# Moving the issue of one value load from SyncE's queue to ScalarE's, in a one-core attention and MLP kernel

## The chip, the cores and the metric

The kernel runs on one core of one Trainium2 chip. The metric is device time in microseconds (us), lower is better. PE is TensorE, ACT is ScalarE, DVE is VectorE, POOL is GpSimd and SP is SyncE; a "q" behind a name (SPq, ACTq) marks the instructions by which that engine issues DMAs.

## The reference

Attention over 4 batches, 8 heads, 768 positions and a head size of 64, and then a two-layer MLP on its 3072 tokens:

```
scores = q @ k^T / 8          # per batch and head, 768 x 768
heads 0, 2, 6 ("retrieval"):  causal mask
heads 1, 3, 4, 5, 7 ("streaming"): causal, and only the first 4 keys or the last 64
a = softmax(scores); x = a @ v          # heads side by side: 3072 x 512
h = x @ w_in                            # 512 -> 2048
out = (max(h, 0) + alpha * min(h, 0)) @ w_out   # 2048 -> 512
```

Inputs and output are float32; inside, the kernel multiplies in bfloat16.

## The kernel before

The heads are worked off in pairs, (2, 6), (1, 5), (0, 4), (3, 7), for each of the 4 batches, so there are 16 pairs, n = 0 to 15; batch 0 holds pairs 0 to 3. For each pair the kernel loads queries (`Lq`), keys (`Lk`) and values (`Lv`) as float32, casts them to bfloat16 (`Cq`, `Ck`, `Cv`), transposes queries and keys on PE (`Tq`, `Tk`, copied out of PSUM by `tq`, `tk`), multiplies keys with queries into PSUM (`S`), takes the exponential on ACT (`s`), multiplies with the values on PE (`A`), divides by the row sum on DVE (`a`), and transposes the result into the MLP's layout (`X`, `x`). The MLP is `P` (first layer), `p` and `g` (activation on ACT and DVE), `O` (second layer) and `o` (output).

The order of all this is written out by hand: `ORDER` (line 14) is one list of items, and the loop at line 807 emits them in that order. An engine executes its own instructions in the order in which they were emitted; engines wait for each other through semaphores only. An item name such as `s0.1.0` reads: exponential, pair 0, second head, part 0.

What the change and the prediction touch:

- `load_v(n)` (line 227) calls `load_rows` (line 230), which issues one DMA for each of the pair's two heads, on SP. Pair 2 is heads 0 and 4. Head 0's values are 128 x 6 x 64 float32 (192 KB), and head 4's are 128 x 7 x 64 float32 (224 KB): a streaming head is cut into 7 tiles, each 124 rows behind the one before it. Both are cut into runs of 256 bytes.
- All loads of queries, keys and values are issued on SP, but for one: the first head's keys of pair 0, on ACT (line 223). ACT also issues the small load of the slopes (line 727) in front of it, and, in the last microseconds, two output tiles.
- In `ORDER`, `Lv2` stands behind `Lq3` (the fourth pair's queries) and in front of `Lv3`. On SP's queue this gives: Lv1 (two DMAs), Lq3 (one), Lv2 (two), Lv3 (two), Lq5, Lk4, and so on.
- `E_retr` (line 466) and `E_stream` (line 513) are the exponentials. In batch 0 the scores of a part take a pair of PSUM banks, and there are two such pairs, `SC2 = [(0, 1), (2, 3)]` (line 292). An exponential gives its pair of banks back, so the scores two parts further on wait for it.
- `cast_v` (line 347) casts the values of pairs 0 to 2 on POOL, and for a streaming head copies the four sink rows into the other tiles (`sinks`, line 301). POOL also casts the queries and keys of pairs 1 to 3, and issues the loads of the MLP's weights (line 693).
- DMAs from SP and ACT use eight completion semaphores in turn, and each waits until the DMA that last used its semaphore is complete.

On ACT the exponentials around the change stand in this order: `s1.1.0`, `s1.0.0` (pair 1), then `s0.1.0`, `s0.1.1`, `s0.1.2` (pair 0, second head), then the copy `tq2`. On PE, the scores `S0.1.2` need the banks that `s0.1.0` gives back, and `A0.1` multiplies what the three exponentials wrote.

Of the kernel before, what the change touches and what calls it, by code (L numbers as in the profile page):

```python
# [14 lines left out]
vz2 id busy warm4 warm0 warm5 vz0 qz0 Lq0.0 sz2 so2 Lq0.1 zero vz3 nms Lk1 Lq1 sz1 Cq0.1 nmr Ck1.1 kz1 La Lk0 Ck1.0  # L15
kz0 Cq1 Cq0.0 Tq0.0 Ck0.0 Tk0.0 tk0.0 Lk2 Ck2.0 Lv0 warm2 tq0.0 S0.0.0 s0.0.0 qz S0.0.1 Tk1 warm3 warm6 vo kz2 Ck0.1
vz1 Ck2.1 Tq1 s0.0.1 tq1 Tq0.1 tk1.1 S0.0.2 s0.0.2 Cv0 tk1.0 m4.0.2 warm7 tq0.1 Lq2 S1.1.0 Tk0.1 tk0.1 S1.0.0 ro0
s1.1.0 Tk2 tk2.1 idf Cq2 s1.0.0 S0.1.0 s0.1.0 A0.0 S0.1.1 s0.1.1 S0.1.2 Tq2 warm8 s0.1.2 tq2 S1.1.1 s1.1.1 A0.1 kz3
sz0 Lk3 Ck3.1 Lv1 S1.0.1 m4.1.2 a0.0 s1.0.1 Al Ck3.0 Lq3 tk2.0 Tk3 S2.0.1 s2.0.1 a0.1 tk3.1 al X0 x0 S2.0.2 Lv2 Lv3
so1 so0 Lq5 wi1 s2.0.2 Lk4 m8.0.2 wi0 Cq3 Tq3 S2.0.0 s2.0.0 tk3.0 Cv1 tq3 A1.0 a1.0 Lk5 kfz2 A1.1 a1.1 kfz0 S2.1.0  # L20
S2.1.1 Cv2 s2.1.1 kfz3 wi6 A2.0 a2.0 wi7 S3.1.0 s2.1.0 s3.1.0 wi5 wi4 S3.0.0 A2.1 Cv3.0 s3.0.0 X1 S3.1.1 s3.1.1 S3.0.1
a2.1 X2 x1 x2 m8.1.2 near2 Ck4.0 P0.0.0 wi2 s3.0.1 A3.0 Cv3.1 P0.3.0 a3.0 P0.2.0 P0.2.1 A3.1 Ck4.1 Lk7 Lk6 P0.1.0
P0.1.1 P0.0.1 Tk4 tk4.0 Cq5 m14.0.2 a3.1 X3 nz1 tk4.1 x3 Tq5 P0.3.1 tq5 P1.2 p1.2 P1.0 p1.0 g1.0 P0.1.2 wi3 P0.13 Lq4
# [51 lines left out]
def kernel(  # L75
# [13 lines left out]
    nc = tc.nc  # L89
    B, H, S, D = q.shape  # L90
# [76 lines left out]
    vf = [stat.tile([128, 7, 2, 64], fp32, name=f"vf{i}") for i in range(NF)]  # L167
# [25 lines left out]
    def dram(t, offset, dims):  # L193
        return bass.AP(t.tensor, t.offset + offset, dims)

    def heads(n):
        return PAIRS[n % 4]
# [17 lines left out]
    def load_k(n):  # L215
        if n >= CROSS:
            load_rows(n, k, kf)
            return
        for hh, h in enumerate(heads(n)):
            T = row_tokens(n, h)  # L220
            dst = kf[n % NF].rearrange("p a b d -> p (a b d)")[:, 6 * D * hh:6 * D * (hh + 1)]

            (nc.scalar if n == hh == 0 else nc.sync).dma_start(
                dst.rearrange("p (x y) -> p x y", y=T * D),
                dram(k, (n // 4 * H + h) * S * D, [[T * D, 128], [128 * T * D, 6 // T], [1, T * D]]))

    def load_v(n):
        load_rows(n, v, vf)

    def load_rows(n, src, bufs):  # L230

        dst = bufs[n % NF]
        for hh, h in enumerate(heads(n)):
            o = (n // 4 * H + h) * S * D
            if n >= LAY and not RETR[h]:

                end = o + 112 * NT * D > B * H * S * D
                nt = NT - end
                nc.sync.dma_start(dst[NSINK:116, 0:nt, hh, :], dram(src, o, [[D, 112], [112 * D, nt], [1, D]]))
                if end:  # L240
                    nc.sync.dma_start(dst[NSINK:100, 6, hh, :], dram(src, o + 672 * D, [[D, 96], [1, D]]))
                (nc.gpsimd if n == 13 and src is k else nc.sync).dma_start(
                    dst[0:NSINK, :, hh, :], dram(src, o, [[D, NSINK], [0, NT], [1, D]]))
                continue
            nt, step = (6, 128) if RETR[h] else (7, 124)
            nc.sync.dma_start(dst[:, 0:nt, hh, :], dram(src, o, [[D, 128], [step * D, nt], [1, D]]))


    ident = const.tile([128, 128], bf16, name="ident")
# [37 lines left out]
    def item(name, fn, *args):  # L287
        I[name] = lambda: fn(*args)
# [67 lines left out]
    def to_array(key, nat, choices, first_half=False):  # L356

        held[key] = take(*choices)
        tr = bank_bf(held[key][0])
        for i in range(6):  # L360
            if first_half:
                nc.tensor.transpose(tr[0:D, 128 * i:128 * (i + 1)], nat[:, i, 0:D], ident)  # L362
            else:
                nc.tensor.transpose(tr[:, 128 * i:128 * (i + 1)], nat[:, i, :], ident)  # L364
# [382 lines left out]
    for n in range(NSEG):  # L747
        if n:
            item(f"Lq{n}", load_q, n)
            item(f"Cq{n}", cast_q, n)  # L750
        item(f"Lk{n}", load_k, n)
        item(f"Lv{n}", load_v, n)
        if n == 3:
            for hh in range(2):
                item(f"Cv{n}.{hh}", cast_v_head, n, hh)
        else:
            item(f"Cv{n}", cast_v, n)
        if n < CROSS:
            for hh in range(2):
                item(f"Ck{n}.{hh}", cast_k, n, hh)  # L760
            if n:
                two = [(4,), (5,)] if n < 4 else ANY
                item(f"Tq{n}", lambda n=n, two=two: to_array(("q", n), natq[n], two))
                item(f"tq{n}", put_q, ("q", n), n, slice(0, 128), "A")
                item(f"Tk{n}", lambda n=n, two=two: to_array(("k", n), natk[n], two))
                for hh in range(2):
                    item(f"tk{n}.{hh}", put_k, ("k", n), n, hh, True)
        else:
            item(f"Ck{n}", cast_k_near, n)
            item(f"Dq{n}", dma_q, n)  # L770
            for hh in range(2):
                item(f"Dk{n}.{hh}", dma_k, n, hh)
        for hh, h in enumerate(heads(n)):
            k_ = (3 if n < 4 else 6) if RETR[h] else (2 if n < 4 else 3)
            for m in range(k_):
                item(f"S{n}.{hh}.{m}", S_retr if RETR[h] else S_stream, n, hh, m)
                item(f"s{n}.{hh}.{m}", E_retr if RETR[h] else E_stream, n, hh, m)
                if n >= 4:
                    item(f"m{n}.{hh}.{m}", M_retr if RETR[h] else M_stream, n, hh, m)
            item(f"A{n}.{hh}", AV, n, hh)  # L780
            item(f"a{n}.{hh}", AV_out, n, hh)
        if LAY <= n < NSEG - 1:
            item(f"X{n}", X_dma, n)
        else:
            item(f"X{n}", X_pe, n)
            item(f"x{n}", X_out, n)
# [61 lines left out]
```

## Time and profile before

| | us |
|---|---|
| median of 3 runs | 228.52 |
| lowest and highest run | 228.26 and 229.8 |
| the profiled execution, its own time | 228.43 |
| its span, from the first to the last instruction | 225.8 |
| PE busy in the span | 221.6 (98%) |
| DVE, ACT, POOL busy | 149.1, 140.1, 45.9 |

The profiled execution's own time is 2.6 us longer than its span; that part lies around the instructions and is in every run. Times in the views below count from the start of the span. The change is in the stretch from 13 to 18 us of the span. In a row of the timeline the first number is when the instructions begin, the second how long they take (a merged row: from the first begin to the last end), then engine, line and operation, with the tiles written and read; behind it, in brackets, how long the engine was idle before and what ended that. The row of an instruction that issues a DMA is the time of the issue, not of the transfer.

### The profile page before, as it was taken

The page shows a single profiled execution, that of the slowest core. Times are in us where ns is not written, and L with a number is a line of the kernel's source. Part 1 is how long each engine was busy: PE and PEld are TensorE (multiplying, and loading weights), DVE is VectorE, ACT ScalarE, POOL GpSimd, SP SyncE. Part 2 cuts the span into 40 slices and gives each one's busy share as a digit, 9 for nine tenths or more (in the row PEclk, how much of TensorE's full clock was granted, in tenths as well). Part 3 has the DMA queues.
Part 4 walks back from the last instruction along what each step waited for, and adds up shares of the span by engine and source line. Part 5 has one row for each costly group of instructions (what it writes and reads, how often), then busy time and mean ns, then how long its engine had stood idle before and what let it go on. Part 6 is the DMA issues. An engine that isn't in the chain of part 4 may idle for free.

```text
span 225.8 us, 5241 instructions
## 1 busy us (share of the span) xinstructions
PE 221.6 (98%) x2005; PEld 136.5 (60%) x2005; DVE 149.1 (66%) x393; ACT 140.1 (62%) x286; POOL 45.9 (20%) x91
## 2 busy tenths in 40 slices
PE   7999999999999999999999999999999999999994
PEld 7989876575556557564556455456556555664454
DVE  5798648986659618897899029977486536866000
ACT  3788669999898036587992147786584237563311
POOL 5679749600230001000400001000110100000000
PEclk9999999999999999999999999999999999999999
DMA  6999999999999999999989999976924420000213
GB/s 201 311 240 214 281 223 285 197 196 231 204 284 182 117 232 231 170 167 190 268 160 177 226 243 129 238 156 117 119 94 38 120 93 0 0 3 1 93 68 119
DMA packets 95417, 37.39 MB, mean 166 GB/s; under 512 B 82440, under 2 KB 93600, under 8 KB 95392
## 3 DMA queue, kind: packets, MB, share of 16 engines
q1 hardware_dynamic: 89136, 27.73, 65.2%
q0 software_dynamic: 5792, 8.93, 17.5%
q10 hardware_dynamic: 464, 0.40, 0.6%
q8 instruction: 15, 0.25, 0.5%
q14 instruction: 10, 0.08, 0.1%
HBM read 27.71 MB, written 6.29 MB: 151 GB/s over the span
## 4 chain that ended last, share of the span: by engine, by line
PE 98%; DVE 0%; issue 0%; DVEq 0%
PE P L598 37%; PE P L618 36%; PE P L553 7%; PE P L431 4%; PE P L414 3%; PE P L688 3%; PE P L364 2%; PE P L637 2%; PE P L424 1%; PE P L502 1%; PE P L578 1%; PE P L463 0%; PE P L362 0%; DVE kT L387 0%; DVE ot L646 0%
## 5 line engine op out<-in xcount | busy, mean ns | idle before, releaser
L610 DVE SCALAR_TENSOR_TENSOR g<-neg,oma,P 128x256 bf16<-128x256 f32 (+1 forms) x128 | 70.9, 608 | 36.9 <-ACT neg L603 36.4
L598 PE MATMUL P<-xT,w_in_b 128*128 128x512 bf16 (+1 forms) x512 | 86.6, 326 | 0.0
L618 PE MATMUL P<-w_out_b,g 128*128 128x512 bf16 x368 | 85.3, 379 | 0.0
L603 ACT ACTIVATE neg<-P 128x512 f32<-128x512 f32 x96 | 54.2, 600 | 26.3 <-PE P L598 20.9
L598 PEld LDWEIGHTS <-w_in_b 128*128 128x128 bf16 x512 | 49.5, 98 | 32.3 <-DVE g L610 0.2
L618 PEld LDWEIGHTS <-g 128*128 128x128 bf16 x368 | 33.9, 98 | 37.2 <-issue 1.0
L470 ACT ACTIVATE eR<-P 128x448 bf16<-128x448 f32 (+4 forms) x63 | 36.9, 635 | 5.8 <-PE P L431 2.5
L624 ACT COPY ot<-P 128x512 f32<-128x512 f32 x23 | 13.9, 605 | 37.1 <-PE P L618 32.3
L628 POOL DMA_DIRECT2D out_dram<-ot x18 | 10.3, 572 | 111.0 <-ACT ot L624 110.8
L518 ACT ACTIVATE eS<-P 128x352 bf16<-128x352 f32 x45 | 20.8, 489 | 3.4 <-PE P L431 3.0
L564 DVE TENSOR_TENSOR xn<-P,rcp 128x448 bf16<-128x448 f32 (+1 forms) x32 | 19.5, 608 | 1.1
L529 DVE TENSOR_TENSOR eS<-eS,ms_near 128x352 bf16<-128x352 bf16 x45 | 14.9, 346 | 0.6 <-ACT eS L518 0.5
L563 DVE RECIPROCAL rcp<-P 128x7 f32<-128x7 f32 (+1 forms) x32 | 6.3, 198 | 10.9 <-PE P L553 10.8
L480 DVE TENSOR_TENSOR eR<-eR,mr_near 128x128 bf16<-128x128 bf16 (+5 forms) x54 | 10.7, 227 | 4.3 <-ACT eR L470 4.1
L414 PE MATMUL P<-qT,kT 128*128 128x192 bf16 (+14 forms) x68 | 11.2, 251 | 0.2 <-DVE kT L387 0.2
L553 PEld LDWEIGHTS <-eS 128*128 128x128 bf16 x260 | 9.5, 97 | 2.3 <-issue 0.6
L553 PE MATMUL P<-vb,eS 128*128 128x65 bf16 x260 | 10.7, 193 | 0.0
L431 PE MATMUL P<-qT,kT 64*128 64x176 bf16 (+10 forms) x168 | 10.5, 252 | 0.0
L431 PEld LDWEIGHTS <-kT 64*128 64x128 bf16 x168 | 6.7, 94 | 6.2 <-issue 5.5
L553 PE MATMUL P<-vb,eR 128*128 128x65 bf16 x276 | 10.5, 193 | 0.0
L553 PEld LDWEIGHTS <-eR 128*128 128x128 bf16 x276 | 9.5, 97 | 1.3
L646 DVE COPY ot<-P 128x128 f32<-128x128 f32 x1 | 0.3, 291 | 14.3 <-PE P L637 14.3
(95 smaller groups left out, 177.3 us busy)
## 6 DMA issues: line engine op xcount, KB each, us to landing
out_dram<-ot POOLq DMA_DIRECT2D x18, 256.0 KB, 3.9
kf<-in_k_dram SPq DMA_DIRECT2D x21, 192.0 KB
qf<-in_q_dram SPq DMA_DIRECT2D x18, 192.0 KB
vf<-in_v_dram SPq DMA_DIRECT2D x14, 196.0 KB
qf<-in_q_dram SPq DMA_DIRECT2D x7, 384.0 KB
vf<-in_v_dram SPq DMA_DIRECT2D x12, 192.0 KB
w_in_b<-in_moe_w_in_dram POOLq DMA_DIRECT2D x8, 256.0 KB, 9.6
w_out_b<-in_moe_w_out_dram POOLq DMA_DIRECT2D x4, 512.0 KB, 13.9
```

The source lines that it names most:

```text
L414: nc.tensor.matmul(to, keys, queries, start=True, stop=stop)
L431: nc.tensor.matmul(to, keys[own], queries[own], start=True, stop=True)
L470: nc.scalar.activation(ebuf[n, hh][:, lo:hi].rearrange("p (x c) -> p x c", x=len(parts)), P[:, got[0]:got[0] + len(parts), 0:(hi - lo) // ...
L518: nc.scalar.activation(slots, sc[:, 0:352].rearrange("p (s c) -> p s c", c=176), AF.Exp, scale=scale)
L529: nc.vector.tensor_tensor(slots, slots, ms_near[:, 0:2, :] if m == 0 else ms_near[:, 1:3, :], op=ALU.mult)
L553: nc.tensor.matmul(pav[:, i, :], e[:, o:o + 128], vv[:, j, hh, 0:D + 1], start=(m == 0), stop=(m == len(terms) - 1))
L564: nc.vector.tensor_tensor(xn[n][:, 0:nt, D * hh:D * hh + D], pav[:, :, 0:D], rcp.to_broadcast([128, nt, D]), op=ALU.mult)
L598: nc.tensor.matmul(psg[:, w * i:w * (i + 1)], w_in_b[:, c, 128 * fb:128 * (fb + 1)], xT[:, c, o:o + w], start=(x == 0), stop=(x == 3))
L603: nc.scalar.activation(neg[t, f], bank(held["P", t, f][0]), AF.Relu, scale=-1.0)
L610: nc.vector.scalar_tensor_tensor(g_buf[t % 2][:, fb, 0:w], neg[t, f][:, c], oma[:, fb:fb + 1], bank(got[0])[:, c], op0=ALU.mult, op1=ALU.add)
L618: nc.tensor.matmul(bank(held["O", t, s][0]), g_buf[t % 2][:, f, 128 * s:128 * (s + 1)], w_out_b[:, f, :], start=(f == 0), stop=(f == 15))
L624: nc.scalar.copy(ot, bank(got[0]))
```

## The change

The load of pair 2's values is split into two items, one for each head. The first head's (`Lv2.0`) keeps its place in the list and its queue. The second head's (`Lv2.1`, 224 KB) is issued by ACT instead of SP, and stands in the list directly in front of `s0.1.0`, which puts it between `s1.0.0` and `s0.1.0` on ACT. Nothing else moves: PE, DVE and POOL have the same instructions in the same order. The moved DMA keeps its completion semaphore, the one that the second head's values of pair 0 (`Lv0`) used before it, and has to wait for that load and for nothing else.

```diff
 ORDER
-s1.1.0 Tk2 tk2.1 idf Cq2 s1.0.0 S0.1.0 s0.1.0 A0.0 ...
+s1.1.0 Tk2 tk2.1 idf Cq2 s1.0.0 S0.1.0 Lv2.1 s0.1.0 A0.0 ...
...
-... X0 x0 S2.0.2 Lv2 Lv3
+... X0 x0 S2.0.2 Lv2.0 Lv3
...
-    def load_v(n):
-        load_rows(n, v, vf)
+    def load_v(n, of=range(2)):
+        load_rows(n, v, vf, of)

-    def load_rows(n, src, bufs):
+    def load_rows(n, src, bufs, of=range(2)):
         dst = bufs[n % NF]
-        for hh, h in enumerate(heads(n)):
+        for hh in of:
+            h = heads(n)[hh]
...
             nt, step = (6, 128) if RETR[h] else (7, 124)
-            nc.sync.dma_start(dst[:, 0:nt, hh, :], dram(src, o, [[D, 128], [step * D, nt], [1, D]]))
+            (nc.scalar if (n, hh) == (2, 1) else nc.sync).dma_start(
+                dst[:, 0:nt, hh, :], dram(src, o, [[D, 128], [step * D, nt], [1, D]]))
...
-        item(f"Lv{n}", load_v, n)
+        if n == 2:
+            for hh in range(2):
+                item(f"Lv{n}.{hh}", load_v, n, [hh])
+        else:
+            item(f"Lv{n}", load_v, n)
```

More of the change, by code (lines that the diff above doesn't have):

```diff
@@ L17 @@
 vz1 Ck2.1 Tq1 s0.0.1 tq1 Tq0.1 tk1.1 S0.0.2 s0.0.2 Cv0 tk1.0 m4.0.2 warm7 tq0.1 Lq2 S1.1.0 Tk0.1 tk0.1 S1.0.0 ro0
-s1.1.0 Tk2 tk2.1 idf Cq2 s1.0.0 S0.1.0 s0.1.0 A0.0 S0.1.1 s0.1.1 S0.1.2 Tq2 warm8 s0.1.2 tq2 S1.1.1 s1.1.1 A0.1 kz3
-sz0 Lk3 Ck3.1 Lv1 S1.0.1 m4.1.2 a0.0 s1.0.1 Al Ck3.0 Lq3 tk2.0 Tk3 S2.0.1 s2.0.1 a0.1 tk3.1 al X0 x0 S2.0.2 Lv2 Lv3
-so1 so0 Lq5 wi1 s2.0.2 Lk4 m8.0.2 wi0 Cq3 Tq3 S2.0.0 s2.0.0 tk3.0 Cv1 tq3 A1.0 a1.0 Lk5 kfz2 A1.1 a1.1 kfz0 S2.1.0
+s1.1.0 Tk2 tk2.1 idf Cq2 s1.0.0 S0.1.0 Lv2.1 s0.1.0 A0.0 S0.1.1 s0.1.1 S0.1.2 Tq2 warm8 s0.1.2 tq2 S1.1.1 s1.1.1 A0.1
+kz3 sz0 Lk3 Ck3.1 Lv1 S1.0.1 m4.1.2 a0.0 s1.0.1 Al Ck3.0 Lq3 tk2.0 Tk3 S2.0.1 s2.0.1 a0.1 tk3.1 al X0 x0 S2.0.2 Lv2.0
+Lv3 so1 so0 Lq5 wi1 s2.0.2 Lk4 m8.0.2 wi0 Cq3 Tq3 S2.0.0 s2.0.0 tk3.0 Cv1 tq3 A1.0 a1.0 Lk5 kfz2 A1.1 a1.1 kfz0 S2.1.0
 S2.1.1 Cv2 s2.1.1 kfz3 wi6 A2.0 a2.0 wi7 S3.1.0 s2.1.0 s3.1.0 wi5 wi4 S3.0.0 A2.1 Cv3.0 s3.0.0 X1 S3.1.1 s3.1.1 S3.0.1
```

## The prediction

> **What bounds the kernel now.** I read the page first: its chain of work that ended last, and then the same chain in order of time, to see how closely PE's instructions follow each other where the change is made and much later.
>
> ```profile
> PE 98%; DVE 0%; issue 0%; DVEq 0%
> ```
>
> ```profile
> 26.67 1.08 PE P L598 x5
> ...
> 28.14 0.86 PE P L598 x4
> ```
>
> ```profile
> 130.50 16.44 PE P L598 x92
> ```
>
> PE makes up 98% of the chain. Four first-layer matmuls at 28.14 us take 0.86 us, five at 26.67 take 1.08, both 0.215 us each; no other group in the chain that I looked at runs at a faster pace for that size (the 92 at 130.50 mix the 512-column and the 256-column form, 0.179 each). So already at 26 us PE is at the pace that it keeps for the rest of the run. Two things follow. A load that lands earlier is worth nothing unless PE is waiting for it; and a stall of PE in the stage of the change is added to the end, as nothing behind it can be made up. The next view is therefore the timeline of the stage, engine by engine: ACT, PE, SP and POOL.
>
> ```profile
> 12.22 0.81 ACT L524 ACTIVATE eS<-P 128x768 bf16<-128x768 f32 x1 [0.18 <-PE P L502]
> 13.39 0.92 ACT L470 ACTIVATE eR<-P 128x896 bf16<-128x896 f32 x1 [0.36 <-PE P L463]
> 14.46 1.73 ACT L470 ACTIVATE eR<-P 128x896 bf16<-128x896 f32 x2 [0.15 <-PE P L463]
> 16.07 0.81 ACT L369 COPY qT<-P 128x768 bf16<-128x768 bf16 x1
> ```
>
> ```profile
> 14.20 0.22 PE L463 MATMUL P<-nmr,ident 128*128 128x128 bf16 x1
> 14.36 0.35 PE L414 MATMUL P<-qT,kT 128*128 128x128 bf16 x2
> ...
> 15.81 0.96 PE L553 MATMUL P<-vb,eR 128*128 128x65 bf16 x21
> ```
>
> The ACT rows are s1.0.0, then s0.1.0, then s0.1.1 with s0.1.2, then tq2. The moved DMA goes between the first two. ACT is idle there for 0.36 us, and again for 0.15 before s0.1.1. On PE, the row at 14.36 is part of the scores S0.1.2. It begins 0.16 us behind the row before it, and s0.1.0, which gives its banks back, ends at 13.39 + 0.92 = 14.31: PE is already waiting for this exponential, with no slack. The row at 15.81 is A0.1: 21 matmuls in 0.96 us, where the same 21 of A0.0 take 0.80 at 13.19; the 0.16 are a wait for s0.1.2.
>
> ```profile
> 9.48 2.06 SPq L246 DMA_DIRECT2D vf<-in_v_dram  x2
> 11.58 2.26 SPq L209 DMA_DIRECT2D qf<-in_q_dram  x1
> 13.88 3.32 SPq L246 DMA_DIRECT2D vf<-in_v_dram  x4
> ```
>
> ```profile
> 0.81 0.42 ACTq L288 DMA_DIRECT2D alpha_r<-in_moe_alpha_dram  x1
> 0.81 0.86 SPq L288 DMA_DIRECT2D qf<-in_q_dram  x2
> 1.26 0.44 ACTq L223 DMA_DIRECT2D kf<-in_k_dram  x1
> ```
>
> SP issues almost without a pause, and its issues are of very unequal length. At the start two take 0.86 us together. Lq3 takes 2.26, from 11.58 to 13.84, though it has nothing left to wait for: it is held up. ACT comes to the moved issue at 12.22 + 0.81 = 13.03, in the middle of that. ACT's own two issues took 0.42 and 0.44, beside SP's, when nothing held either of them up.
>
> ```profile
> 13.50:14.00 0.50, 0.50 (x18) 0.42 (x14) 0.49 (x2) 0.50 (x1) 0.50 (x2) 1.00 1.08 176
> 14.00:14.50 0.50, 0.50 (x6) 0.36 (x5) 0.50 (x3) 0.35 (x2) 0.50 (x2) 1.00 0.43 80
> 14.50:15.00 0.50, 0.50 (x10) 0.45 (x9) 0.47 (x4) 0.50 (x1) 0.50 (x2) 1.00 1.08 114
> ```
>
> The last column is GB/s moved by DMA: 176, 80 and 114, where the half microseconds from 10.5 to 12 moved over 300. While SP is held up in Lq3 the DMA engines run dry.
>
> **The change part by part.** *SP loses one issue.* Seen alone, Lv2.1 is the row from 14.40 to 14.94, so 0.54 us. SP's later issues can start up to 0.54 us earlier. The first time that any engine waits for one of those loads is POOL at 25.80, for keys, after 1.27 us of idleness. PE reaches what POOL casts there at 28.84, straight from P L598 at full pace. The gain to the end is 0; what hides it is PE's own work.
>
> *The values come earlier.* POOL casts them (Cv2) at 19.69, without a wait. Gain 0.
>
> *The DMA of 224 KB shares the engines with what SP has queued.* At the 307 GB/s of 11.5 to 12.0 it is worth 229 KB / 307 = 0.75 us, so Lk3, Lv1 and Lq3 can land 0 to 0.75 us later. POOL casts Lq3 at 17.04 and Lv1 at 17.80 to 18.8, and its two sink copies end at 19.45. PE takes the queries at 18.92, 1.03 us behind the end of the cast at 17.89, and begins A1.0 at 19.75, 0.30 behind the second sink copy. Bounds: 0, and 0.75 - 0.30 = 0.45 if all of it reaches POOL and the first matmul needs both copies. It needs only the first head's, so I take 0. If PE is itself late by 0.45 or more, this is hidden.
>
> *ACT gains one issue.* It does not wait for its semaphore: pair 0's values had landed when POOL cast them at 11.06. The trace has no ACT issue while SP is held up, so the length is bounded. From below: 0.44, ACT's own row for a load of keys. Then ACT is free at 13.47 instead of 13.39, and s0.1.0 is 0.08 late, which the idle 0.15 behind it takes up: 0 at the end. From above: 2.41, the longest SP issue before this point (Lq2, from 5.91). Then ACT is free at 15.44, 2.05 late. Between: ACT is held until SP is through, at 13.84, and then needs its own 0.44: 14.28, so s0.1.0 is 0.89 late. I take this one. The row nearest in time is SP's own issue beside it, which is held up then, and the two ACT rows come from a moment in which no issue was.
>
> *What is queued behind it.* s0.1.0 ends at 14.28 + 0.92 = 15.20. S0.1.2 on PE is 0.89 late. s0.1.1 begins at 15.20 instead of 14.46: 0.74, since the idle 0.15 is used up. s0.1.2 and tq2 follow back to back, 0.74 late. A0.1 arrives 0.89 late at its wait, of which 0.16 exist already; s0.1.2 lets it go 0.74 late. So PE loses 0.74 us here, and behind it has nothing that could absorb it. POOL, DVE and SP are then early in relation to PE, and wait a little longer.
>
> Sum: 0 + 0 + 0 + 0.74. On the profiled execution's own time: 228.43 + 0.74 = 229.17. The profiled time is 0.09 below the median of the runs shown, 228.52. I say **229.2 us**, 0.3% slower than before, which is inside the 1% that a measurement of this kernel can tell from no change.
>
> The Trainium skill, Perfetto Trace Analysis, section DMA Instruction — HWDGE (DVE, Sync), says that a DMA of this kind first takes an exclusive lock on a descriptor generator, and that the time until it has the lock is inside the recorded issue. By that rule ACT would wait for the end of Lq3, and the sum would be the 229.2; without it, by ACT's own row, 228.5. The start of this trace shows both queues issuing at once with no sign of the lock (0.42 beside 0.86 for two), so no row here decides it.
>
> **The rivals.** *ACT is not held up.* For it: 0.42 and 0.44 beside SP's issues. Against: no issue was held up then. It gives 228.43 + 0 to 0.1, so about 228.5, not slower; with all of the late landing, 228.9. It decides once the issue takes less than 13.39 + 0.15 - 13.03 = 0.51 us.
>
> *SP gets the next turn as well.* SP's following issue begins only 0.04 us behind Lq3 and lasts 0.47, until 14.35. If ACT comes after it, it ends at 14.79, s0.1.0 is 1.40 late and PE 1.25: 229.7.
>
> *ACT is held for as long as the longest issue,* because its own descriptors do not fit: 2.05 late, PE 1.90, 230.3, with 2.68 (the longest issue in the first 30 us) 230.6. Only with some further loss would this pass 230.8, over 1%.
>
> *A gain.* PE's waits in the stage, 0.16 at 14.20 to 14.36 and 0.16 in A0.1, are for ACT, which the change cannot make earlier. If the earlier loads removed as much elsewhere: 228.1. Against it: from 15 to 35 us PE shows no idle time at all.
>
> **How the numbers follow.** Held until SP is through: 0.48. Not held: 0.34. SP has the next turn as well: 0.09. Held for the longest time: 0.06, half of it or less beyond 1%. A gain: 0.03. The likeliest gives 229.2; its own range is 229.0 to 229.4. The range of 228.3 to 229.8 takes in the first three cases. Faster by over 1% has 0.01, as no row offers 2.3 us; slower by over 1% has 0.03; within 1% is 0.96.
>
> **What would show it.** In the profile after: an ACTq row of line 247 from 13.03 with 1.2 to 1.3 us (right) or about 0.5 (not held); s0.1.0 at 14.3 and not 13.4; the row of S0.1.2 at 15.2; A0.0 to A0.1 drawn out; DMA still below 180 GB/s in 13.5 to 15 if held, near 300 if not. A cast of Lq3 on POOL behind a wait for DMA would show the shared engines. The prediction is wrong if the ACTq row is short, or if it is long and PE's later groups still begin at their old times.

## The result and the profile after

| | before | after |
|---|---|---|
| median of 22 runs each, us | 228.30 | 228.95 |
| lowest and highest run, us | 227.35 and 231.08 | 228.49 and 230.6 |
| ratio, with its 95% interval | | 1.0041 [1.0023, 1.0059] |
| the profiled execution's own time, us | 228.43 | 229.06 |

The change costs 0.4%, about 0.9 us. Of the experiments below, the profiles of the extra copy and of the load later on ACT are of slow runs, which every ratio leaves out (the medians do not): of these two profiles what waits for what is read, and a size in them is that of one execution. Line 246 of the code is line 247 in the changed kernel, and the lines behind it are numbered 2 higher (8 higher in the two kernels with parts of the load).

ACT's timeline around the moved issue, after:

```profile
11.84 0.81 ACT L526 ACTIVATE eS<-P 128x768 bf16<-128x768 f32 x1 [0.18 <-PE P L504]
11.85 0.42 ACTq L247 DMA_DIRECT2D vf<-in_v_dram  x1
12.67 0.92 ACT L472 ACTIVATE eR<-P 128x896 bf16<-128x896 f32 x1
```

The issue is short, 0.42, and it lies wholly inside the exponential `s1.0.0`: it begins 0.01 us behind it and is over 0.38 us before that ends. `s0.1.0` follows at 12.67 with no idle time at all. So the issue takes nothing from ACT. SP's timeline shows that SP was held up in Lq3 at the same moment:

```profile
11.79 1.66 SPq L209 DMA_DIRECT2D qf<-in_q_dram  x1
```

The loss is on POOL and then on PE. POOL's timeline shows the cast of Lq3, here before:

```profile
17.04 0.85 POOL L315 CAST g<-qf 128x768 bf16<-128x768 f32 x1
```

And after, with the two sink copies of Lv1, which follow behind the cast of Lv1:

```profile
18.46 0.83 POOL L317 CAST g<-qf 128x768 bf16<-128x768 f32 x1 [1.67 <-DMA qf<-in_q_dram]
...
20.23 0.63 POOL L308 COPY vb<-vb 4x192 f32<-4x192 f32 x2
```

Before, the cast found its queries there. After, POOL was idle for 1.67 us and a DMA into `qf` ended that: the cast begins 1.42 us later (18.46 against 17.04). By the trace's DMA records the last packet of Lq3 ended at 17.80 instead of 16.46, so 1.34 later; the cast began 0.66 us behind it, and 0.58 in the kernel before, where Lq3 was thus only just in time. All that POOL does behind it moves by the same 1.4 us. Now PE's timeline, before and then after: Tq3 (the row with `g`), A1.0 and the scores behind it. After, the last group ahead of Tq3 stands in front; before, the same group began at 18.86.

```profile
18.92 0.50 PE L364 MATMUL P<-ident,g 128*128 128x128 bf16 x6
...
19.75 0.95 PE L553 MATMUL P<-vb,eS 128*128 128x65 bf16 x26
20.54 0.24 PE L414 MATMUL P<-qT,kT 128*128 128x192 bf16 x1
```

```profile
18.14 0.23 PE L465 MATMUL P<-nmr,ident 128*128 128x144 bf16 x1
19.34 0.51 PE L366 MATMUL P<-ident,g 128*128 128x128 bf16 x6 [0.97 <-POOL g L317]
...
20.22 0.22 PE L555 MATMUL P<-vb,eS 128*128 128x65 bf16 x2
20.62 0.89 PE L555 MATMUL P<-vb,eS 128*128 128x65 bf16 x24 [0.18 <-POOL vb L308]
21.34 0.24 PE L416 MATMUL P<-qT,kT 128*128 128x192 bf16 x1
```

Before, PE goes from group to group and does the 26 matmuls of A1.0 in one piece. After, it waits twice: 18.14 to 19.34 for Tq3, 1.14 us more than the 0.06 step between the same two groups before, and inside A1.0 from 20.22 to 20.62, after two matmuls, until the first sink copy is done. The second wait is 0.40 - 0.06 = 0.34.

The two waits add up to 1.48, but PE is only 0.80 behind at the next group (21.34 against 20.54). It had come to this place 0.72 us earlier than before (18.14 against 18.86). That is jitter of the first loads: in two experiments with the same work in front, below, the same group began at 18.56 (five tiles) and 19.43 (values cast first). It is also worth nothing here, since A1.0 cannot go on until POOL's copy is ready at 20.6, however early PE stands there. So the sum is simple. The copy is ready 2.12 us behind the start of the cast of Lq3 (20.23 + 0.35 = 20.58, from the row below, less 18.46). With the cast at 17.04 that was 19.16, and PE passed this point at about 19.81 (19.75 and two matmuls): slack 0.65. The delay of 1.42 less 0.65 makes 0.77, against 0.80 seen.

The chain of waits of the changed kernel, in order of time, now runs through POOL where it was all PE:

```profile
18.48 0.81 POOL g L317
...
20.23 0.35 POOL vb L308
20.62 0.89 PE P L555 x24
```

And far behind it, the chain's row with 32 second-layer matmuls, which began at 123.59 before:

```profile
124.29 6.91 PE P L620 x32
```

The stall is carried along to the end: 0.70 later here, and also 0.70 later at the last DVE instruction (223.55 against 222.85).

Why Lq3 lands later is seen in the DMA of the stretch from 13.5 to 15.5, in half microseconds (last column GB/s), after:

```profile
13.50:14.00 0.50, 0.50 (x7) 0.40 (x6) 0.47 (x4) 0.35 (x2) 0.50 (x2) 1.00 1.06 207
14.00:14.50 0.50, 0.50 (x12) 0.49 (x10) 0.50 (x2) 0.50 (x1) 0.50 (x2) 1.00 1.33 252
14.50:15.00 0.50, 0.50 (x12) 0.50 (x10) 0.41 (x4) 0.50 (x2) 0.50 (x3) 1.00 1.32 229
15.00:15.50 0.50, 0.50 (x14) 0.40 (x12) 0.50 (x2) 0.50 (x2) 0.50 (x2) 1.00 1.17 235
```

The hole of before (176, 80, 114) is filled, at 231 GB/s on average. What fills it is the 224 KB: by the trace's DMA records ACT's queue moved 169 KB from 14 to 15 us, and SP's 66. The first packet of ACT's queue began at 13.33, the first of Lq3 at 14.83. Two things in this are easily missed. The load on ACT was not issued ahead of Lq3: its issue began 0.06 us behind Lq3's (11.85 and 11.79), and it overtook Lq3 on its own queue. And its transfer did wait: the first packet came 1.06 us behind the end of its issue (12.27), at about the time at which SP's issue of Lq3 ended (13.45).

### The profile page after: what moved, and what is told of

Read it like the earlier page. It is cut to its first block, busy times and chain, and to the rows that moved or that the text cites. A ratio compares the mean times of both kernels' runs of the same rounds, so it can differ in the third digit from the quotient of the medians.

```text
span 226.9 us, 5213 instructions
## 1 busy us (share of the span) xinstructions
PE 219.5 (97%) x1977; PEld 135.8 (60%) x2005; DVE 149.6 (66%) x393; ACT 140.3 (62%) x286; POOL 46.1 (20%) x91
## 4 chain that ended last, share of the span: by engine, by line
PE 89%; DMA 3%; POOL 3%; SPq 2%; issue 2%; DVE 0%; POOLq 0%; DVEq 0%
PE P L600 36%; PE P L620 35%; PE P L555 7%; PE P L433 4%; DMA qf<-in_q_dram 3%; PE P L639 2%; PE P L426 1%; PE P L366 1%; SPq L223 1%; POOL g L317 1%; PE P L580 1%; PE P L416 1%; PE P L504 1%; POOL w_in_b L695 1%; SPq L247 0%
## 5 line engine op out<-in xcount | busy, mean ns | idle before, releaser
L600 PE MATMUL P<-xT,w_in_b 128*128 128x256 bf16 (+1 forms) x501 | 85.7, 325 | 0.6
L620 PE MATMUL P<-w_out_b,g 128*128 128x512 bf16 x351 | 83.1, 379 | 1.0 <-issue 0.2
```

The costliest lines, as they stand in the source:

```text
L600: nc.tensor.matmul(psg[:, w * i:w * (i + 1)], w_in_b[:, c, 128 * fb:128 * (fb + 1)], xT[:, c, o:o + w], start=(x == 0), stop=(x == 3))
L620: nc.tensor.matmul(bank(held["O", t, s][0]), g_buf[t % 2][:, f, 128 * s:128 * (s + 1)], w_out_b[:, f, :], start=(f == 0), stop=(f == 15))
```

## The experiments

The theory after the result: what costs time is that 224 KB are served in front of Lq3, on whatever queue; Lq3 lands later, POOL casts it later, and PE waits at Tq3 and A1.0. The rivals: ACT pays for issuing a DMA (as the prediction had it); or a second queue takes more than its share of the DMA engines from SP's.

**Only an issue, and nothing to move.** To the kernel before, an extra load of 8 KB on ACT at the same place.

```diff
+    item("La2", nc.scalar.dma_start, extra, moe_alpha...)    # 16 x 128 float32
-s1.0.0 S0.1.0 s0.1.0
+s1.0.0 S0.1.0 La2 s0.1.0
```

> The kernel before, with one more DMA on ACT in front of s0.1.0, of 8 KB (the slopes again, into a spare tile that nobody reads). All loads stay on SP. Theory (shared DMA engines): an issue of about 0.42 us on ACT that delays nothing, ratio 1.000 within 0.002. Rival (the issue on ACT costs): ratio 1.003 to 1.005 with s0.1.0 late by 0.1 us or more.

228.28 us, ratio 1.0006 [0.9975, 1.0037]. The issue and the exponential behind it, in ACT's timeline:

```profile
12.42 0.33 ACTq L288 DMA_DIRECT2D extra<-in_moe_alpha_dram  x1
13.24 0.92 ACT L470 ACTIVATE eR<-P 128x896 bf16<-128x896 f32 x1
```

SP was inside its own issue of Lq3 (12.10 to 13.81). The issue costs ACT nothing in these rows, so the rival that ACT pays falls; the interval by itself does not exclude its 1.003.

**Only the traffic.** To the kernel before, an extra copy of the same 224 KB on ACT at the same place, into a tile that nobody reads; Lv2 stays on SP.

```diff
+    item("Lx", nc.scalar.dma_start, extra, dram(v, 4 * S * D, [[D, 128], [124 * D, 7], [1, D]]))
-s1.0.0 S0.1.0 s0.1.0
+s1.0.0 S0.1.0 Lx s0.1.0
```

> The kernel before, with all its loads on SP, and a second copy of the same 224 KB issued on ACT in front of s0.1.0 into a spare tile that nobody reads. It takes nothing off SP. Theory (shared DMA engines): Lq3 lands 1 us or more later, PE waits at Tq3 for POOL's cast by 0.7 to 1.5 us, ratio 1.003 to 1.007, no better than the change. Rival (what costs is that SP's later loads come in another order): no wait at Tq3, ratio 1.000 to 1.002.

229.08 us, ratio 1.0066 [1.0033, 1.0099]. POOL's timeline:

```profile
18.70 0.83 POOL L315 CAST g<-qf 128x768 bf16<-128x768 f32 x1 [1.75 <-DMA qf<-in_q_dram]
...
29.61 0.50 POOL L328 CAST natm<-kf 128x384 bf16<-128x384 f32 x1 [3.15 <-DMA kf<-in_k_dram]
```

The traffic alone brings the whole delay of the cast. PE waits 0.31 us more than usual at Tq3, less than expected because it came there later, and 0.34 at A1.0. In this profile the cast of keys at 29.61 waits 3.15 too; that the 224 KB which the kernel does not need are the cause is not shown, as the kernel before with `Lq3` first (below) waits 2.61 at the same cast without them.

**The same position on SP's queue.** The changed kernel with the moved load on SP, in front of Lq3.

```diff
-            (nc.scalar if (n, hh) == (2, 1) else nc.sync).dma_start(
+            nc.sync.dma_start(
-S0.1.0 Lv2.1 s0.1.0
+S0.1.0 s0.1.0
-Ck3.0 Lq3
+Ck3.0 Lv2.1 Lq3
```

> The moved load goes back to SP, but in front of Lq3 instead of behind Lv2's first head: the early place without ACT. Theory (224 KB served in front of Lq3, whatever the queue): Lq3 lands 0.7 to 1.5 us later than in the kernel before, PE waits at Tq3, ratio 1.003 to 1.008. Rival (a second queue beside SP's takes an unfair share of the DMA engines, and in one queue there is no harm): ratio 1.000 to 1.002.

228.98 us, ratio 1.0049 [1.0021, 1.0078], against 1.0041 of the changed kernel. POOL's timeline, and then PE's:

```profile
18.81 0.83 POOL L317 CAST g<-qf 128x768 bf16<-128x768 f32 x1 [1.59 <-DMA qf<-in_q_dram]
```

```profile
20.97 0.88 PE L555 MATMUL P<-vb,eS 128*128 128x65 bf16 x24 [0.18 <-POOL vb L308]
```

Without ACT, and with one queue, the loss is the same within the intervals. So the loss needs no second queue, and what matters is that the 224 KB are served in front of Lq3. On ACT it is the second queue that brings them there, since they are issued behind Lq3: by 0.06 us in the changed kernel, by 1.14 with the extra copy (12.59 and 11.45). The rival falls as the cause of the loss, but whether ACT's queue also takes more than its share is not settled.

**Lq3 out of the way.** The changed kernel with Lq3 in front of Lv1 on SP, so that it is issued before the moved load; and the kernel before with the same swap, to see what the swap is worth by itself.

```diff
-sz0 Lk3 Ck3.1 Lv1 S1.0.1 m4.1.2 a0.0 s1.0.1 Al Ck3.0 Lq3 tk2.0
+sz0 Lk3 Ck3.1 Lq3 Lv1 S1.0.1 m4.1.2 a0.0 s1.0.1 Al Ck3.0 tk2.0
```

> The changed kernel, with the fourth pair's queries Lq3 issued on SP in front of Lv1 instead of behind it. The moved load stays on ACT where the change put it. Theory (PE pays only because Lq3 lands behind the 224 KB): Lq3 lands 1 us or more earlier, POOL's cast of it no longer waits, PE begins Tq3 without idleness, and the time goes back to that of the kernel before or a little below, ratio 0.997 to 1.001. Rival (the 224 KB delay every load by the same amount, so some other wait takes its place, Lv1 first): a wait of PE in A1.0 of 0.5 to 1 us, ratio 1.003 to 1.005.

> The kernel before, with Lq3 in front of Lv1 on SP; all loads on SP. It separates the swap's own worth from what it mends in the changed kernel. Theory: in the kernel before Lq3 is only just in time, so the swap is worth 0 to 0.3 us in most executions, ratio 0.997 to 1.001. Rival (the swap is good or bad in itself): ratio below 0.997 or above 1.003.

With the change 228.34 us, ratio 1.0022 [0.9996, 1.0049]; without it 228.29, 1.0019 [0.9989, 1.0050]. POOL in the kernel with the change:

```profile
16.95 0.85 POOL L317 CAST g<-qf 128x768 bf16<-128x768 f32 x1
```

The cast has no wait, PE none at Tq3 and A1.0, and with the swap on both sides the change no longer shows in the time (1.0022 beside 1.0019). The two intervals together leave about 0.9 us open between these two, as much as the change costs, so it is the rows that show it more than the times. Both ratios lie above the 0.997 to 1.001 that had been expected: the swap may cost something itself, but both intervals hold 1.

**Parts of the load.** The changed kernel, but ACT issues only the first three tiles (96 KB), or the first five (160 KB); SP issues the others behind `Lv2.0`.

```diff
-            for hh in range(2):
-                item(f"Lv{n}.{hh}", load_v, n, [hh])
+            item("Lv2.0", load_v, n, [0])
+            item("Lv2.1", load_v, n, [1], (0, 3))       # or (0, 5), on ACT
+            item("Lv2.1r", load_v, n, [1], (3, 7))      # or (5, 7), on SP
```

> The changed kernel, with only three of the seven tiles (96 of 224 KB) on ACT at the early place, the other four (128 KB) on SP behind Lv2's first head. Theory (bytes in front of Lq3): about three sevenths of the delay, Lq3 0.4 to 0.7 us late instead of 1.4, PE's wait at Tq3 0 to 0.5 us, ratio 1.001 to 1.003. Rival (one more queue costs, whatever its size): ratio 1.004 as with the change.

> The changed kernel, but ScalarE issues only five of the seven tiles of the moved load (160 of 224 KB) at the early place; SyncE issues the other two behind Lq3. Theory of the shared engines (Lq3 lands later by what is served in front of it): with 96 KB the cast of Lq3 began 0.5 us later than before (17.53), with 224 KB 1.42 us later (18.46), so by interpolation 160 KB puts it near 18.0, behind a wait for DMA of about 1.2 us. That is 0.95 us late against PE's slack of 1.03 at Tq3: PE waits there for at most 0.2 us, and at A1.0 for 0.1 to 0.35 behind the sink copies. Ratio 1.000 to 1.003. Rival (the cost hangs on how many loads stand in front, and not on their size): cast as late as in the changed kernel, 18.4 or later, PE waits 1 us and 0.34, ratio 1.004.

Three tiles: 227.94 us, ratio 0.9984 [0.9958, 1.0011]. Five: 228.30, 0.9999 [0.9970, 1.0028]. POOL with three tiles, then with five, and PE with five (timelines):

```profile
17.53 0.83 POOL L323 CAST g<-qf 128x768 bf16<-128x768 f32 x1 [0.52 <-DMA qf<-in_q_dram]
```

```profile
18.23 0.83 POOL L323 CAST g<-qf 128x768 bf16<-128x768 f32 x1 [1.46 <-DMA qf<-in_q_dram]
```

```profile
20.39 0.89 PE L561 MATMUL P<-vb,eS 128*128 128x65 bf16 x24 [0.18 <-POOL vb L314]
```

The cast moves with the size, and the price begins only when the slack is used up. With 96 KB the copy is ready at 17.53 + 2.12 = 19.65, before PE's 19.81: no cost is due, and none is measured, where a tenth of a per cent or more had been expected. With 160 KB this profile stands at 20.39, so 0.58 late; the runs give 0.00, with up to 0.6 us inside the interval. That the cost at 160 KB is smaller than at 224 is likely, though the two intervals touch (up to 1.0028, and from 1.0023 on); its size is open. The cast had been expected near 18.0 and began at 18.23.

**Queries on ACT, values on SP.** The kernel before with Lq3 issued by ACT in front of `s0.1.0`.

```diff
-            item(f"Lq{n}", load_q, n)
+            item(f"Lq{n}", load_q, n, nc.scalar if n == 3 else nc.sync)
-S0.1.0 s0.1.0
+S0.1.0 Lq3 s0.1.0
```

> All values on SP as in the kernel before, and Lq3 itself issued on ACT, in front of s0.1.0, where the change puts the values. Its runs are of 1536 bytes, the values' of 256. Theory (the two queues are served packet by packet, so the queue with the longer runs gets the larger share): Lq3 lands earlier than in the kernel before although it is issued later, no wait at Tq3, ratio 0.996 to 1.001. Rival (ACT's queue comes after what SP has queued): Lq3 late by 0.5 us or more, a wait at Tq3, ratio 1.002 to 1.006.

228.19 us, ratio 1.0023 [1.0000, 1.0045]. A miss: Lq3 does not land earlier. POOL's timeline:

```profile
18.10 0.83 POOL L315 CAST g<-qf 128x768 bf16<-128x768 f32 x1 [0.82 <-DMA qf<-in_q_dram]
```

Here Lv2 follows Lv1 on SP without Lq3 between, so more of the values go out at the same time as Lq3. A queue of its own bought the queries nothing here.

**Values cast first.** The changed kernel, with the cast of Lv1 in front of the cast of Lq3 on POOL.

```diff
-Cq3 Tq3 S2.0.0 s2.0.0 tk3.0 Cv1 tq3
+Cv1 Cq3 Tq3 S2.0.0 s2.0.0 tk3.0 tq3
```

> The changed kernel with Cv1 (pair 1's values) in front of Cq3 on GpSimd, so that it uses the time in which Cq3 waits for the late Lq3. Theory of the shared engines: the cast of Lq3 still begins at about 18.5, as its wait for DMA ends, so PE still waits 0.9 to 1.1 us at Tq3; the second sink copy of pair 1 ends 0.8 us earlier, so the wait of 0.34 at A1.0 goes. Ratio 1.002 to 1.004, against 1.004 of the changed kernel. Rival (the loss comes from GpSimd being late as a whole, and not from the landing of Lq3): the loss vanishes, ratio 1.000.

228.50 us, ratio 1.0020 [0.9989, 1.0050]. POOL's timeline:

```profile
18.54 0.82 POOL L317 CAST g<-qf 128x768 bf16<-128x768 f32 x1 [0.26 <-DMA qf<-in_q_dram]
```

POOL now casts and copies Lv1 from 16.63 to 18.28, while Lq3 is under way, yet the cast of Lq3 still begins at 18.54, when it lands. A1.0's wait is gone, as expected. The expected wait at Tq3 is not in this profile, because PE came there only at 19.50, 0.14 behind the end of the cast; by PE's time of before (18.92) it would be 0.44. The time lies where the theory put it, but its interval holds the rival's 1.000 as well.

**Later on ACT.** The changed kernel with the moved load further on in ACT's order, between `tq2` and `s1.1.1`, when SP has already queued Lq3.

```diff
-S0.1.0 Lv2.1 s0.1.0
+S0.1.0 s0.1.0
-S1.1.1 s1.1.1
+S1.1.1 Lv2.1 s1.1.1
```

> The moved load stays on ACT, but stands in front of the exponential s1.1.1, behind the copy tq2, some 4 us later. Theory (the 224 KB are served in front of the fourth pair's queries Lq3, which then land late, and PE waits for their cast on POOL): Lq3 is home by then, so no wait of PE at Tq3 and the time of the kernel before, ratio 0.998 to 1.001. Rival (an additional DMA issue on ACT costs by itself): ratio 1.004 as with the change. Rival (the two profiles differ by chance in when loads land): also a wait at Tq3 now and then, ratio anywhere from 1.000 to 1.004.

233.09 us, ratio 1.0100 [1.0052, 1.0147]: a miss, though not of the theory's first half. POOL's timeline, and then PE's:

```profile
17.00 0.83 POOL L317 CAST g<-qf 128x768 bf16<-128x768 f32 x1 [0.36 <-DMA qf<-in_q_dram]
...
25.80 0.93 POOL L351 CAST vb<-vf 128x896 bf16<-128x896 f32 x1 [6.11 <-DMA vf<-in_v_dram]
```

```profile
26.78 0.43 PE L555 MATMUL P<-vb,eR 128*128 128x65 bf16 x5 [5.05 <-POOL vb L351]
```

Lq3 is on time now, and nothing is lost at Tq3 or A1.0. But the values, issued from 15.47 to 15.86, land 10 us later, and PE waits 5.05 for them. Before, the same values were issued on SP from 14.40 to 14.94, and cast at 19.69 without a wait. Why the load is so slow on ACT's queue at that moment is not settled; what moves beside it are the loads of the weights, which POOL issues from 15.23 on, and SP's row of loads.

There is a second cost behind the wait. A line of the profile's page gives the clock that was granted to PE, in tenths, for 40 equal slices of the span; here it is for this kernel, and then for the extra copy:

```profile
PEclk9999799999999999999999999999999999999999
```

```profile
PEclk9999997999999999999999999999999999999999
```

By the trace's clock records the granted clock was 0.50 for 3.41 us, from 26.24 us on, around the end of the wait of 5.05. With the extra copy it was 0.50 for 3.41 us from 33.77 on, behind a wait of PE of 2.83. No other profile has such a stretch while PE is at work, and none has a wait of PE over 1.1 us. That the wait brings the clock down fits this, but no run tests it. It matters for the size: eight of the 12 runs of this kernel have a mean granted clock of 0.985 to 0.993, as this one has (0.993), against two of the 35 of the kernel before that ran beside them. The ratio rests on five of the 12 runs, four of them without it, and so understates what this place costs: the medians of all runs are 233.09 and 228.05.

The kernels that move the same data as before and cast Lq3 ahead of Lv1, with Lv1 ahead of Lq3 on the queues. The release is the cast's start and 2.12, the loss by rows is the release less 19.81, and the loss by runs is the ratio less one, times 228.3:

| kernel | cast of Lq3 begins | release | loss by rows, us | loss by runs, us |
|---|---|---|---|---|
| before | 17.04 | 19.16 | 0 | |
| three tiles on ACT | 17.53 | 19.65 | 0 | -0.4 (-1.0 to 0.3) |
| queries on ACT | 18.10 | 20.22 | 0.41 | 0.5 (0 to 1.0) |
| five tiles on ACT | 18.23 | 20.35 | 0.54 | 0.0 (-0.7 to 0.6) |
| after | 18.46 | 20.58 | 0.77 | 0.9 (0.5 to 1.3) |
| on SP, ahead of Lq3 | 18.81 | 20.93 | 1.12 | 1.1 (0.5 to 1.8) |

Each row is one profiled execution, so the agreement is within what the first loads' jitter allows, and it says no more than that. The 19.81 is from one profile as well: in the seven profiles in which PE does A1.0 in one piece, it begins it between 19.61 and 20.35, 19.97 in the middle. From that middle the loss by rows after the change is 0.55 instead of 0.77, which the runs (0.5 to 1.3) hold too, so the closeness of 0.77 to 0.80 in one pair of profiles is partly chance. No version is shown to be faster than the kernel before.

## Why the prediction came out as it did

The forecast of 229.2 lies 0.25 above the median of 228.95, and the direction is right. That is luck, as the mechanism is not right: the 0.74 that made the forecast was not there, and a term that it took as 0 was worth about 0.8. The base was less firm than it looks, too: the 2.6 us around the instructions, which the forecast carries along, are not in every run; in most of the 22 runs after they are 1.7, and 3.0 at most.

- *What bounds the kernel.* Right. PE has nothing behind this stage that could make up a stall, and the 0.70 were still there at 124 us and at the end.
- *SP loses one issue: 0.* Right; it brought nothing that PE waited for. *The values come earlier: 0.* Right, for the same reason.
- *ACT gains one issue: held to 14.28, PE 0.74 late.* This is the step that failed. The issue took 0.42 while SP was held up, and 0.33 to 0.45 in the eight experiments that issue a load on ACT around there. It also did not begin behind `s1.0.0`, as the prediction had it (13.03), but beside it. So the condition of the rival, under 0.51, was met with a margin that the prediction had not seen: the issue does not stand in ACT's row at all. By the Trainium skill, Perfetto Trace Analysis, section DMA Instruction — HWDGE (DVE, Sync), the issue should have had to wait for an exclusive lock on the descriptor generator, and that wait should have been in its recorded time. In the recorded time these rows do not agree with that: 0.42 on ACT, inside 1.66 on SP. What was held is the transfer, and not ACT: in seven of the nine kernels with such an issue the first packet on ACT's queue came within 0.3 us of the end of the issue that SP was in (13.33 and 13.45 here, 14.09 and 13.81 with the 8 KB), in the other two 1.3 and 2.2 us behind it. Whether that is the lock, waited for behind the recorded issue, or the order in which the packets are served stays open.
- *The 224 KB share the engines: between 0 and 0.45, taken as 0.* The mechanism is the one that decided, and it was described to the instruction: POOL's cast, the first sink copy, A1.0. Its sizes were off twice. The landing was put at up to 0.75 late, from 307 GB/s; the stretch moved 231, by which 229 KB take 0.99, and the delay was 1.34 by the packets and 1.42 at the cast, of which the last 0.35 to 0.43 is not accounted for. The slack was put at 0.30 behind the second sink copy, with the remark that only the first is needed; that remark was right, and makes the slack 0.65. With 0.75 - 0.65 the term would have been 0.1; with the measured delay of the cast it is 0.77.
- *Rival "not held up".* Its second figure, 228.9 "with all of the late landing", is what happened, nearly to the tenth, but not by its sum: its 0.45 is 0.75 less 0.30, and the runs showed 1.42 less 0.65.
- *The hole in the DMA from 13.5 to 15* was read as spare time. It was filled (207, 252, 229, between the two signs that the prediction named), but in front of Lq3, which SP was issuing until 13.45. The Trainium skill, DMA: Bandwidth & Descriptors, section Issuing engines are not separate DMA queues, says that DMAs started by several engines run on the same 16 DMA engines, and that a second issuer only saves time on the sequencer. The pair of runs agrees: 1.0041 with the load on ACT and 1.0049 with it on SP, both served ahead of Lq3.

## What to carry to other kernels

A load that is started earlier is paid for by the loads that it overtakes, and on a second queue these can be loads that were issued before it: name the one that is then last, and count from its landing through every consumer to the first point where the bounding engine needs it, with the slack at that point. Take the delay from the rate that the DMA engines reach on such runs in that very stretch, not from the best half microsecond near it, and take it as a lower bound (here 0.99 of 1.34). When the bounding engine has passed a point early by chance, a release that comes from a DMA takes that away again, so the price is release less the usual passing time, not the sum of the waits in one profile.

## What the runs showed of the hardware that was not expected

- A DMA issue on ACT ran beside a running exponential: it began at 11.85 within the one from 11.84 to 12.65, and cost the next one nothing.
- ACT's issue was not held up while SP's was: 0.42, 0.33 and 0.39 us on ACT (after, with the 8 KB, with three tiles), each inside SP's issue of Lq3, which took 1.66, 1.71 and 3.30. The transfers were: their first packets came at 13.33, 14.09 and 13.96, near the end of SP's issue (13.45, 13.81 and 13.93).
- In the one profile of the load later on ACT, 224 KB on ACT's queue, issued at 15.47, had their last packet at 25.19 and were cast at 25.80, although the DMA engines moved 200 to 340 GB/s in that time. Why they were served so late stays open.
- PE's granted clock was 0.50 for 3.41 us around or behind waits of PE of 5.05 and 2.83 us, in two profiles; in the other ten PE waits 1.1 us at most, and the clock is 1.00 while it is at work.
